# Filler products between the row groups of the first batch, and a softmax that works by rows of the score matrix

## The chip, the cores and the metric

The kernel runs on one core of one Trainium2 chip. The metric is the device time of one execution in microseconds (us), and the number given for a kernel is the median of its runs. A core has five engines with a queue of instructions each: TensorE (PE in the profile; its weight loads are listed apart as PEld), VectorE (DVE), ScalarE (ACT), GpSimd (POOL) and SyncE (SP). Each works through its queue in order and waits on semaphores for the others. Here POOL and SP do little but issue DMA transfers.

## The reference, cut to what matters

There are 4 batches of N = 6016 rows and C = 256 columns for each of q, k and v. Attention is between columns, not rows. After it comes a gated feed-forward layer with 1536 inner columns.

```
qn = q / (norm(q, axis=1) + 1e-6)        # one norm for each batch and column
kn = k / (norm(k, axis=1) + 1e-6)
s  = kn.T @ qn / tau                     # 256 x 256 for each batch, tau = 1
a  = exp(s - max(s));  a /= a.sum(-1) + 1e-9
x  = v @ a
out = (sigmoid(x @ w_gate) * (x @ w_val)) @ w_out
```

## The kernel before

**What is multiplied.** The kernel never forms x. Since x @ w_gate = v @ (a @ w_gate), it computes two small matrices for each batch, G = a @ w_gate and H = a @ w_val (256 x 1536 each). The large loop then multiplies the transposed v by G and H. The numerators of the softmax are held transposed in `x_sb` and `e_sb`: the partitions are columns of q, in two halves j of 128, and the free dimension is columns of k, in two blocks i of 128. A sum over a row of a is therefore a sum over partitions, made by PE with a vector of ones. The row maximum is replaced by the bound 1/tau.

**Rows.** The 6016 rows are 47 tiles of 128. Four tiles make a chunk, so a batch has 12 chunks (`ci` 0 to 11), the last one with 3 tiles. For the first batch, `groups0` has eleven groups of 4 tiles, then one of 2 and one of 1.

**The main loop** (L478 to L499) runs over batches b, chunks ci and twelve steps f. `glu` (L334) computes 128 inner columns for a whole chunk: two matmuls into `ps_gate`, two into `ps_val`, a sigmoid on ACT into `g_sb` (L353), and their product on DVE into `hT` (L354). The second matmul layer, `out_mms` (L360), lies one chunk behind: four of its matmuls follow each step, and after every twelfth `flush` (L376) copies a finished `ps_o` on DVE in the next step (L380). In chunks 9 and 10 of the first three batches ("block") these 48 matmuls come after the twelve steps instead of between them.

**Side work** (`side_work`, L433) is a table written by hand. While batch b runs, it gives the steps in which the pieces of batch b+1 are issued, after that step's `glu` and `out_mms`. The slot ci*12 + f names chunk and step. Loads and scores are spread over chunks 0 to 8. Then come, before the change: the norms' products in chunk 9, step 10, and the square root in step 11 (L462, L463); `norms_inv`, add and reciprocal on DVE, in chunk 10, step 1 (L464); two copies of the scores out of PSUM, `copy_s`, in step 2 (L466); `spread_k`, four PE products that lay the inverse norms of k along a row of `ps_rk`, in step 4 (L467); `scale_k` for both blocks in step 6 and `exps` in step 11 (L469, L470); `sums` for both blocks in chunk 11, step 0 (L471); and the twelve products `gh` (L292) in chunk 11, one in each of the steps 1 to 10 and two in step 11 (L474). A `gh` product is two matmuls into a `ps_gh`, then a copy out of PSUM that multiplies by the inverse row sum `rrow`, on ACT (L307) or DVE (L309).

**The softmax before.** `scale_k(b, i)` makes two DVE instructions of 128 columns, multiplying by both inverse norms: `r` (q, one for each partition) and `ps_rk` (k). `exps(b, i)` is one exp over both halves j of column block i. `sums(b, i)` is two matmuls with the ones into a `ps_r`, then an add (L280) and a reciprocal (L281) on DVE. The products are ordered by `gh_order` = (fg, i, w): fg is one of three groups of 512 inner columns, w is gate or val.

**PSUM.** There are eight buffers: psg 2 (`ps_gate`), psv 2 (`ps_val`), pso 2 (`ps_o`, `ps_rk`), pss 1 (scores) and psm 1 (norms and others). A tile that takes a buffer waits for the last reader of the tile before it. Sums and products of the side work alternate between psm and pss.

**The head** (L391 to L430). POOL's queue loads batch 0's groups of q and k, then v and the weights. For each group g come the squares, on DVE for q and ACT for k (exchanged for the last group), the scores, and then the norms' products of group g-1. `sqpool` holds two squares of each kind, so a square waits for the norms' products two groups back. After the last group come the square root, `norms_inv`, `copy_s`, twelve unread products by `busy` (L385: 128-column products of ones with ones, into a psg buffer), `spread_k`, four more, `scale_k` and `exps` for both blocks, the transposes of the first v chunk on PE, whose two halves DVE and ACT copy (L328, L329), and six `gh` products into psg, psv and pso. The other six follow the first six steps of chunk 0. `transpose_v(0, 1)` is also made on PE, in step 7 of chunk 0; all later chunks of v are transposed by DMA. A table load for exp (L405) and one for the sigmoid (L425) are placed by hand on ACT.

```
    for g in range(last0 + 2):
        if g <= last0:
            ...
            for u in range(nt):
                score(0, t0, u)
        if g >= 1:
            norm_mms(ps_n0, sq.pop(g - 1), groups0[g - 1][1], g == 1, g == last0 + 1, (0, 1) if g <= last0 else (1, 0))
```

Of the kernel before, what the change touches and what calls it, by code (L numbers as in the profile page):

```python
# [9 lines left out]
FP32 = mybir.dt.float32  # L10
BF16 = mybir.dt.bfloat16
# [6 lines left out]
def kernel(  # L18
# [68 lines left out]
    def mm(out, lhsT, rhs, start, stop, **kw):  # L87
        nc.tensor.matmul(out, lhsT=lhsT, rhs=rhs, start=start, stop=stop, **kw)  # L88
# [82 lines left out]
            )  # L171
        return sq

    def norm_mms(ps, sqs, nt, first, last, order=(0, 1)):

        for w in order:
            sq = sqs[w]
            for u in range(nt):
                for j in range(CB):
                    mm(  # L180
                        ps[:, w * CB + j : w * CB + j + 1],
                        sq[:, u, ds(j * P, P)],
                        ones_bf[:, 0:1],
                        start=(first and w == order[0] and u == 0 and j == 0),
                        stop=(last and u == nt - 1),
                        skip_group_check=True,
                    )
# [59 lines left out]
            s["x"] = attp.tile([P, CB, C], FP32, tag="x", name="x_sb")  # L247
        nc.vector.tensor_copy(out=s["x"][:, j, :], in_=s["s"][:, j, :])

    def scale_k(b, i):  # L250

        s = st[b]
        for j in range(CB):
            x = s["x"][:, j, ds(i * P, P)]
            nc.vector.scalar_tensor_tensor(  # L255
                out=x,
                in0=x,
                scalar=s["r"][:, j : j + 1],
                in1=s["rk"][:, ds(i * P, P)],
                op0=ALU.mult,  # L260
                op1=ALU.mult,
            )

    def exps(b, i):

        s = st[b]
        e = attp.tile([P, CB, P], BF16, tag=f"e{i}", name=f"e_sb{i}", bufs=2)
        nc.scalar.activation(  # L268
            out=e, in_=s["x"][:, :, ds(i * P, P)], func=ACT.Exp, bias=shift
        )  # L270
        s.setdefault("e", []).append(e)
        s.setdefault("rrow", [])

    def sums(b, i, pl=psm, tag="m"):
        s = st[b]
        ps_r = pl.tile([P, 1], FP32, tag=tag, name="ps_r")
        for j in range(CB):
            mm(ps_r, s["e"][i][:, j, :], ones_bf[:, 0:1], j == 0, j == CB - 1)
        r = attp.tile([P, 1], FP32, tag=f"rrow{i}", name="rrow", bufs=2)
        nc.vector.tensor_scalar(out=r, in0=ps_r, scalar1=1e-9, scalar2=None, op0=ALU.add)  # L280
        nc.vector.reciprocal(r, r)  # L281
        s["rrow"].append(r)

    def gh_tiles(b):
        st[b]["gh"] = [
            [ghpool.tile([P, CB, FG], BF16, tag=f"{n}{fg}", name=f"gh_{n}{fg}") for fg in range(NFG)]
            for n in ("G", "H")
        ]

    gh_order = [(fg, w, i) for fg in range(NFG) for i in range(CB) for w in range(2)]  # L290

    def gh(b, n, pl=None, tag=None, act=None):  # L292
        s = st[b]
        fg, w, i = gh_order[n]
        ps = (pl or psm).tile([P, FG], FP32, tag=tag or "m", name="ps_gh")
        for j in range(CB):
            mm(
                ps,
                s["e"][i][:, j, :],
                w_sb[w][fg][:, j, :],  # L300
                start=(j == 0),
                stop=(j == CB - 1),
            )
        dst = s["gh"][w][fg][:, i, :]
        r = s["rrow"][i]
        if act if act is not None else n % 2 == 0:
            nc.scalar.activation(out=dst, in_=ps, func=ACT.Copy, scale=r)  # L307
        else:
            nc.vector.tensor_scalar(out=dst, in0=ps, scalar1=r, scalar2=None, op0=ALU.mult)  # L309
# [1 line left out]

    vts = {}

    def transpose_v(b, ci, ps=None, late=None):

        t0, nt = groups[ci]
        v_sb = vs.pop((b, ci))
        vT = vtpool.tile([P, TPC * CB, P], BF16, tag="vT", name="vT")
        flat = v_sb[:, :nt, :].rearrange("p t c -> p (t c)")
        if ps is None:  # L320
            nc.sync.dma_start_transpose(out=vT[:, : nt * CB, :], in_=flat)
        else:
            for n in range(nt * CB):
                nc.tensor.transpose(
                    out=ps[:, n, :], in_=flat[:, ds(n * P, P)], identity=ident_bf
                )
            half = nt * CB // 2
            nc.vector.tensor_copy(out=vT[:, :half, :], in_=ps[:, :half, :])  # L328
            (nc.scalar.copy if late is None else late)(vT[:, half : nt * CB, :], ps[:, half : nt * CB, :])  # L329
        vts[b, ci] = vT.rearrange("p (u cb) n -> p cb u n", cb=CB)  # L330

    hts = {}
# [52 lines left out]
    def busy(n):  # L385

        ps = psg.tile([P, CH], FP32, tag="g", name="ps_busy")
        for _ in range(n):
            mm(ps[:, :P], ones_bf, ones_bf, True, True)

    ps_n0 = psm.tile([P, 2 * CB], FP32, tag="m", name="ps_n")  # L391
    sq = {}
    last0 = len(groups0) - 1
    for g in range(last0 + 2):
        if g <= last0:
            t0, nt = groups0[g]
            engines = (nc.vector, nc.scalar) if g < last0 else (nc.scalar, nc.vector)
            sq[g] = [squares(0, t0, nt, w, engines[w]) for w in range(2)]
            for u in range(nt):
                score(0, t0, u)  # L400
        if g >= 1:
            norm_mms(ps_n0, sq.pop(g - 1), groups0[g - 1][1], g == 1, g == last0 + 1, (0, 1) if g <= last0 else (1, 0))
    st[0]["n"] = ps_n0
    norms_sqrt(0)
    nc.scalar.preload_act_table(ACT.Exp)  # L405
# [2 lines left out]
    copy_s(0, 1)  # L408
    busy(12)
    spread_k(0)  # L410
    busy(4)
    scale_k(0, 0)
    scale_k(0, 1)
    late = []
    transpose_v(
        0, 0, psv.tile([P, TPC * CB, P], BF16, tag="v", name="ps_tp"), lambda *a: late.append(a)
    )
    exps(0, 0)
    exps(0, 1)
    nc.scalar.copy(*late.pop())  # L420
    gh_tiles(0)
    sums(0, 0)
    gh(0, 0, psg, "g", act=False)
    gh(0, 1, psv, "v", act=True)
    nc.scalar.preload_act_table(ACT.Sigmoid)  # L425
    sums(0, 1, pss, "s")
    gh(0, 2, psg, "g", act=False)
    gh(0, 3, psv, "v", act=False)
    gh(0, 4, pso, "o", act=True)
    gh(0, 5, pso, "o", act=False)  # L430


    def side_work(b):  # L433

        side = {}

        def at(slot, fn, *a):
            side.setdefault(divmod(slot, FC), []).append((fn, a))

        for ci in range(NCH):  # L440
            nb, nci = (b, ci + 1) if ci + 1 < NCH else (b + 1, 0)
            lb, lci = (b, ci + 2) if ci + 2 < NCH else (b + 1, ci + 2 - NCH)
            if (nb, nci) == (0, 1):
                at(7, lambda: transpose_v(0, 1, psm.tile([P, TPC * CB, P], BF16, tag="m", name="ps_tp")))
            elif nb < B:
                at(ci * FC + 2, transpose_v, nb, nci)
            if lb < B:
                at(ci * FC + 0, load_v, lb, lci)
        n = b + 1
        if n == B:  # L450
            return side
        first, last = (14 if b == 0 else 0), 9 * FC
        for g, (t0, nt) in enumerate(groups):
            s0 = first + g * (last - first) // NCH
            at(max(0, s0 - 20), load_qk, n, t0, nt)
            for u in range(nt):
                at(first + (t0 + u) * (last - first) // NT, score, n, t0, u)
            if g == 0:
                at(s0, acc_start, n)
            for i, (fn, w) in enumerate(((acc_square, 0), (acc_add, 0), (acc_square, 1), (acc_add, 1))):  # L460
                at(s0 + 1 + 2 * i, fn, n, g, w)
        at(9 * FC + 10, norms_mm, n)  # L462
        at(9 * FC + 11, norms_sqrt, n)  # L463
        at(10 * FC + 1, norms_inv, n)  # L464
        for j in range(CB):
            at(10 * FC + 2, copy_s, n, j)  # L466
        at(10 * FC + 4, spread_k, n)  # L467
        for i in range(CB):
            at(10 * FC + 6, scale_k, n, i)  # L469
            at(10 * FC + 11, exps, n, i)  # L470
            at(11 * FC + 0, sums, n, i, *((psm, "m"), (pss, "s"))[i])  # L471
        at(11 * FC + 0, gh_tiles, n)
        for i in range(len(gh_order)):
            at(11 * FC + min(i + 1, FC - 1), gh, n, i, *((psm, "m"), (pss, "s"))[i % 2])  # L474
        return side


# [1 line left out]
    for b in range(B):  # L479
        side = side_work(b)  # L480
        for ci in range(NCH):
            block = b + 1 < B and ci in (9, 10)
            for f in range(FC):
                glu(b, ci, f)
                flush()
                if prev is not None and not block:
                    out_mms(*prev, f * TPC, (f + 1) * TPC)
                for fn, a in side.get((ci, f), ()):
                    fn(*a)
                if (b, ci) == (0, 0) and f < len(gh_order) - 6:  # L490
                    gh(0, 6 + f, pso, "o")
            if prev is not None and block:
                for s in range(TPC):
                    out_mms(*prev, s * FC, (s + 1) * FC)
# [40 lines left out]
```

## Time and profile before

| | us |
|---|---|
| median of 3 runs (lowest, highest) | 834.85 (834.69, 836.2) |
| time of the profiled execution | 834.69 |
| its span | 832.8 |
| around the span | 1.9 |

The profile is of one execution. Its page has numbered parts: busy time of each engine; the span in 40 slices of 20.8 us; DMA queues; the chain of work that ended last; groups of equal instructions with mean duration and what their engine waited for; and DMA issues. Two rows of the second part:

```profile
PE   5899999999999999999999999999999999999998
...
DMA  9999623326655543223865453223222523322111
```

Each digit is a share in tenths: PE is less than full in the first two slices and the last, and the DMA engines are full in the first four. Besides the page, the trace answers questions by window. The timeline lists start, duration, engine, line, operation, written tile <- read tiles, shape and count, and in square brackets the idle time of the engine before it and what ended that. The ends of matmuls are modelled and overlap, so the pitch from start to start is the better measure of a stream of them.

### The profile page before, as it was taken

How to read it: one execution, taken by the hardware profiler on the slowest of the kernel's cores; microseconds unless marked ns; L12 is line 12 of the kernel's file. 1: busy time of each engine (PE TensorE's matmuls, PEld its weight loads, DVE VectorE, ACT ScalarE, POOL GpSimd, SP SyncE). 2: the span in 40 equal slices, each digit the busy share in tenths (PEclk: the TensorE clock that was granted, in tenths of full speed). 3: DMA queues.
4: the chain of work that ended last, by engine and by line, in shares of the span. 5: the costliest groups of instructions: out<-in, count | busy, mean ns of one | idle time of the engine just before them, and what ended most of it. 6: DMA issues, size and time to landing. Idle time of an engine off the chain costs nothing.

```text
span 832.8 us, 14005 instructions
## 1 busy us (share of the span) xinstructions
PE 813.2 (98%) x5322; PEld 506.0 (61%) x5332; DVE 568.6 (68%) x993; ACT 390.8 (47%) x642; POOL 82.9 (10%) x159
## 2 busy tenths in 40 slices
PE   5899999999999999999999999999999999999998
PEld 4656666665666666665576666666566566666666
DVE  2477777776667777777657777777766666666664
ACT  4554444445544444444654444444655444444442
POOL 5532100002011100000210020000000000000000
PEclk9799999999999999999999999999999999999999
DMA  9999623326655543223865453223222523322111
GB/s 209 206 206 185 130 52 89 61 52 130 133 102 108 102 106 57 58 52 83 156 130 103 84 113 78 51 75 65 61 48 64 83 51 82 71 48 70 45 35 71
DMA packets 78739, 77.19 MB, mean 93 GB/s; under 512 B 50768, under 2 KB 55632, under 8 KB 78672
## 3 DMA queue, kind: packets, MB, share of 16 engines
q0 software_dynamic: 23920, 38.81, 28.1%
q1 hardware_dynamic: 54608, 36.97, 17.0%
q8 instruction: 41, 0.67, 0.3%
q10 hardware_dynamic: 144, 0.52, 0.2%
q14 instruction: 26, 0.21, 0.1%
HBM read 78.64 MB, written 24.64 MB: 124 GB/s over the span
## 4 chain that ended last, share of the span: by engine, by line
PE 93%; DMA 4%; DVE 1%; issue 0%; POOL 0%; ACT 0%; POOLq 0%
PE ps_o L88 30%; PE ps_gate L88 29%; PE ps_val L88 29%; PE ps_s L88 4%; DMA k_sb<-in_k_dram 3%; PE ps_gh L88 2%; DMA w_val<-in_moe_w_val_dram 1%; DVE hT L354 1%; ACT g_sb L353 0%; DVE x_sb L255 0%; PE ps_rk L88 0%; PE ps_n L88 0%; POOL q_sb L97 0%; POOL w_gate L137 0%; POOL k_sb L97 0%
## 5 line engine op out<-in xcount | busy, mean ns | idle before, releaser
L354 DVE TENSOR_TENSOR hT<-ps_val,g_sb 128x512 bf16<-128x512 f32 (+1 forms) x576 | 390.9, 680 | 211.7 <-ACT g_sb L353 206.7
L353 ACT ACTIVATE g_sb<-ps_gate 128x512 bf16<-128x512 f32 (+1 forms) x576 | 338.5, 588 | 398.6 <-PE ps_gate L88 390.8
L88 PE MATMUL ps_val<-vT,gh_H 128*128 128x512 bf16 (+1 forms) x1152 | 337.8, 375 | 1.5 <-DVE hT L354 1.4
L88 PE MATMUL ps_gate<-vT,gh_G 128*128 128x512 bf16 (+1 forms) x1152 | 337.8, 375 | 0.6 <-ACT g_sb L353 0.3
L88 PE MATMUL ps_o<-w_out_sb,hT 128*128 128x256 bf16 x2256 | 326.4, 273 | 0.0
L88 PEld LDWEIGHTS <-hT 128*128 128x128 bf16 x2256 | 220.7, 98 | 124.8
L88 PEld LDWEIGHTS <-gh_H 128*128 128x128 bf16 x1152 | 112.7, 98 | 132.9 <-issue 2.6
L88 PEld LDWEIGHTS <-gh_G 128*128 128x128 bf16 x1152 | 112.2, 98 | 36.9 <-issue 0.5
L380 DVE COPY out_sb<-ps_o 128x256 f32<-128x256 f32 x188 | 78.2, 416 | 20.6 <-PE ps_o L88 20.6
L106 POOL DMA_DIRECT2D v_sb<-in_v_dram x48 | 25.5, 531 | 626.6 <-DMA vT<-v_sb 513.3
L88 PE MATMUL ps_s<-k_sb,q_sb 128*128 128x256 bf16 x376 | 71.8, 293 | 12.6 <-ACT k_sb L128 7.1
L88 PEld LDWEIGHTS <-q_sb 128*128 128x128 bf16 x376 | 39.1, 104 | 20.4 <-DVE q_sb L127 6.7
L208 DVE TENSOR_TENSOR acc<-acc,sq 128x1024 bf16<-128x1024 bf16 (+1 forms) x66 | 44.2, 670 | 0.0
L169 DVE TENSOR_TENSOR sq<-q_sb 128x1024 bf16<-128x1024 bf16 (+2 forms) x45 | 30.1, 670 | 19.0 <-PE ps_n L88 18.2
L97 POOL DMA_DIRECT2D q_sb<-in_q_dram x48 | 26.2, 547 | 15.7 <-DMA q_sb<-in_q_dram 6.7
L97 POOL DMA_DIRECT2D k_sb<-in_k_dram x48 | 26.4, 549 | 14.0 <-DMA k_sb<-in_k_dram 8.7
L169 DVE TENSOR_TENSOR sq<-k_sb 128x1024 bf16<-128x1024 bf16 (+2 forms) x34 | 22.4, 658 | 0.7 <-PE ps_n L88 0.7
L307 ACT ACTIVATE gh_G<-ps_gh,rrow 128x512 bf16<-128x512 f32 x22 | 15.1, 687 | 13.3 <-PE ps_gh L88 9.1
L167 ACT ACTIVATE sq<-k_sb 128x1024 bf16<-128x1024 bf16 (+1 forms) x12 | 12.3, 1021 | 14.8 <-DMA k_sb<-in_k_dram 12.9
L309 DVE TENSOR_SCALAR gh_H<-ps_gh,rrow 128x512 bf16<-128x512 f32 x23 | 17.1, 743 | 1.8 <-PE ps_gh L88 1.6
L88 PE MATMUL ps_gh<-w_val,e_sb 128*128 128x512 bf16 x45 | 13.6, 379 | 0.5 <-DMA w_val<-in_moe_w_val_dram 0.3
L88 PEld LDWEIGHTS <-e_sb 128*128 128x128 bf16 x112 | 10.1, 97 | 5.3 <-ACT e_sb L268 0.7
(49 smaller groups left out, 92.8 us busy)
## 6 DMA issues: line engine op xcount, KB each, us to landing
out_dram<-out_sb SPq DMA_DIRECT2D x44, 512.0 KB, 2.9
v_sb<-in_v_dram POOLq DMA_DIRECT2D x44, 256.0 KB, 3.8
q_sb<-in_q_dram POOLq DMA_DIRECT2D x43, 256.0 KB, 6.8
k_sb<-in_k_dram POOLq DMA_DIRECT2D x43, 256.0 KB, 7.7
out_dram<-out_sb SPq DMA_DIRECT2D x4, 384.0 KB, 2.5
w_gate<-in_moe_w_gate_dram POOLq DMA_DIRECT2D x3, 256.0 KB, 6.8
w_val<-in_moe_w_val_dram POOLq DMA_DIRECT2D x3, 256.0 KB, 7.4
w_out_sb<-in_moe_w_out_dram POOLq DMA_DIRECT2D x1, 768.0 KB, 12.6
```

The source lines that it names most:

```text
L88: nc.tensor.matmul(out, lhsT=lhsT, rhs=rhs, start=start, stop=stop, **kw)
L97: nc.gpsimd.dma_start(out=tl[:, :nt, :], in_=rows(src, b)[:, t0 : t0 + nt, :])
L106: nc.gpsimd.dma_start(out=v_sb[:, :nt, :], in_=rows(v, b)[:, t0 : t0 + nt, :])
L167: nc.scalar.activation(out=sq[:, :nt, :], in_=src[:, :nt, :], func=ACT.Square)
L169: engine.tensor_tensor(out=sq[:, :nt, :], in0=src[:, :nt, :], in1=src[:, :nt, :], op=ALU.mult)
L208: nc.vector.tensor_tensor(out=acc[:, :nt, :], in0=acc[:, :nt, :], in1=st[b]["sq", w][:, :nt, :], op=ALU.add)
L307: nc.scalar.activation(out=dst, in_=ps, func=ACT.Copy, scale=r)
L309: nc.vector.tensor_scalar(out=dst, in0=ps, scalar1=r, scalar2=None, op0=ALU.mult)
L353: nc.scalar.activation(out=g_sb[:, :n], in_=ps_gate[:, :n], func=ACT.Sigmoid)
L354: nc.vector.tensor_tensor(out=hts[b, ci][:, f, :n], in0=ps_val[:, :n], in1=g_sb[:, :n], op=ALU.mult)
L380: nc.vector.tensor_copy(out=out_sb[:, s, :], in_=ps)
```

## The change

It consists of these parts:

- **Filler in the head.** `busy(40)` stands ahead of the first group. In the group loop `busy(12)` follows the norms' products for g = 0 to 10. After `spread_k` there are ten such products instead of four.
- **Squares of the last group.** Both are on DVE. `norm_mms` loses its parameter for the order, and q always comes first.
- **Softmax by rows.** `scale_k` makes two DVE products of 256 columns with `ps_rk` alone. The inverse norms of q become the per-partition scale of `exps`, which makes one exp for each half j. The sums over a row need both halves; `sums` makes four matmuls into one psm tile, one add and one reciprocal, and takes over the allocation of G and H.
- **Order and buffers of the products.** `gh_order` is (fg, w, i). In the side work sums and products all use psm. In the head, four products precede the loop, into psg and psv, with odd ones copied on ACT; the other eight follow steps 0 to 7 of chunk 0.
- **Copies of the transposed v** in chunks 0 and 1 of batch 0 are one DVE copy.
- **Slots of the side work.** `spread_k` moves from step 4 to 2, `copy_s` from 2 to 1 and `scale_k` from 6 to 4 of chunk 10; product n goes from step n+1 to n of chunk 11.

```diff
-            norm_mms(ps_n0, sq.pop(g - 1), groups0[g - 1][1], g == 1, g == last0 + 1, (0, 1) if g <= last0 else (1, 0))
+            norm_mms(ps_n0, sq.pop(g - 1), groups0[g - 1][1], g == 1, g == last0 + 1)
+        if g < NT // TPC:
+            busy(12)
...
+    def scale_k(b):
         s = st[b]
         for j in range(CB):
+            x = s["x"][:, j, :]
+            nc.vector.tensor_tensor(out=x, in0=x, in1=s["rk"], op=ALU.mult)
+
+    def exps(b):
+        s = st[b]
+        s["e"] = attp.tile([P, CB, C], BF16, tag="e", name="e_sb", bufs=2)
         for j in range(CB):
+            nc.scalar.activation(
+                out=s["e"][:, j, :],
+                in_=s["x"][:, j, :],
+                func=ACT.Exp,
+                bias=shift,
+                scale=s["r"][:, j : j + 1],
+            )
+
+    def sums(b):
+        s = st[b]
+        ps_r = psm.tile([P, CB], FP32, tag="m", name="ps_r")
+        for i in range(CB):
+            for j in range(CB):
+                mm(
+                    ps_r[:, i : i + 1],
+                    s["e"][:, j, ds(i * P, P)],
+                    ones_bf[:, 0:1],
+                    start=(i == 0 and j == 0),
+                    stop=(j == CB - 1),
+                    skip_group_check=True,
+                )
+        r = attp.tile([P, CB], FP32, tag="rrow", name="rrow", bufs=2)
         nc.vector.tensor_scalar(out=r, in0=ps_r, scalar1=1e-9, scalar2=None, op0=ALU.add)
         nc.vector.reciprocal(r, r)
...
-    gh_order = [(fg, w, i) for fg in range(NFG) for i in range(CB) for w in range(2)]
+    gh_order = [(fg, w, i) for fg in range(NFG) for w in range(2) for i in range(CB)]
...
-            half = nt * CB // 2
-            nc.vector.tensor_copy(out=vT[:, :half, :], in_=ps[:, :half, :])
-            (nc.scalar.copy if late is None else late)(vT[:, half : nt * CB, :], ps[:, half : nt * CB, :])
+            nc.vector.tensor_copy(out=vT[:, : nt * CB, :], in_=ps[:, : nt * CB, :])
...
+    busy(40)
     ps_n0 = psm.tile([P, 2 * CB], FP32, tag="m", name="ps_n")
...
-            engines = (nc.vector, nc.scalar) if g < last0 else (nc.scalar, nc.vector)
-            sq[g] = [squares(0, t0, nt, w, engines[w]) for w in range(2)]
+            sq[g] = (
+                squares(0, t0, nt, 0, nc.vector),
+                squares(0, t0, nt, 1, nc.vector if g == last0 else nc.scalar),
+            )
...
-    busy(4)
-    scale_k(0, 0)
-    scale_k(0, 1)
...
+    busy(10)
+    scale_k(0)
+    transpose_v(0, 0, psv.tile([P, TPC * CB, P], BF16, tag="v", name="ps_tp"))
+    exps(0)
     nc.scalar.preload_act_table(ACT.Sigmoid)
-    sums(0, 1, pss, "s")
-    gh(0, 2, psg, "g", act=False)
-    gh(0, 3, psv, "v", act=False)
-    gh(0, 4, pso, "o", act=True)
-    gh(0, 5, pso, "o", act=False)
+    sums(0)
+    for n in range(4):
+        gh(0, n, *((psg, "g"), (psv, "v"))[n % 2], act=1)
...
+        at(10 * FC + 2, spread_k, n)
         for j in range(CB):
-            at(10 * FC + 2, copy_s, n, j)
-        at(10 * FC + 4, spread_k, n)
-        for i in range(CB):
-            at(10 * FC + 6, scale_k, n, i)
-            at(10 * FC + 11, exps, n, i)
-            at(11 * FC + 0, sums, n, i, *((psm, "m"), (pss, "s"))[i])
-        at(11 * FC + 0, gh_tiles, n)
+            at(10 * FC + 1, copy_s, n, j)
+        at(10 * FC + 4, scale_k, n)
+        at(10 * FC + 11, exps, n)
+        at(11 * FC + 0, sums, n)
         for i in range(len(gh_order)):
-            at(11 * FC + min(i + 1, FC - 1), gh, n, i, *((psm, "m"), (pss, "s"))[i % 2])
+            at(11 * FC + i, gh, n, i)
...
-                if (b, ci) == (0, 0) and f < len(gh_order) - 6:
-                    gh(0, 6 + f, pso, "o")
+                if (b, ci) == (0, 0) and f < len(gh_order) - 4:
+                    gh(0, 4 + f, pso, "o", act=1)
```

## The prediction

> **What bounds the kernel now.** I read the page's first two parts, then the list of PE's waits, then PE's busy time in stretches of 3.41 us, then the timeline of the first 55 us and of the change from batch 0 to batch 1.
>
> ```profile
> PE 813.2 (98%) x5322; PEld 506.0 (61%) x5332; DVE 568.6 (68%) x993; ACT 390.8 (47%) x642; POOL 82.9 (10%) x159
> ...
> PEclk9799999999999999999999999999999999999999
> ```
>
> TensorE (PE) is busy in 98% of the span, so a moment in which it waits is added to the time. The granted clock is below full only in the first two slices. PE's own waits, as total, count and longest:
>
> ```profile
> PE ps_s L88 <- ACT k_sb L128: 7.1, 1, 7.1
> PE ps_s L88 <- DMA k_sb<-in_k_dram: 5.5, 8, 2.1
> PE ps_val L88 <- DVE hT L354: 1.4, 3, 0.5
> ```
>
> Up to 32 us PE waits for loads of k. The third row is one wait at each batch change. Now PE in stretches of 3.41 us (busy us, count, granted clock, DMA share, GB/s); the clock changes only at their edges:
>
> ```profile
> 10.09:13.50 3.41, 2.25 (x45) 0.99 1.13 211
> 13.50:16.91 3.41, 3.15 (x30) 0.51 1.12 209
> ...
> 20.33:23.74 3.41, 1.82 (x13) 0.50 1.12 208
> 23.74:27.15 3.41, 2.94 (x43) 0.50 1.12 209
> 27.15:30.57 3.42, 3.15 (x30) 0.51 1.13 207
> 30.57:33.98 3.41, 2.85 (x59) 1.00 1.24 204
> ```
>
> After a full-clock stretch with 2.25 us busy the clock halves. After half-clock stretches with 3.15 us it comes back, after 2.94 it did not, and at full clock 2.85 us kept it. The data rate is 207 to 211 GB/s in both states: the loads set the pace, not the clock. The last stretch begins warm, before the last full group of k lands:
>
> ```profile
> 31.94 1.03 PE L88 MATMUL ps_s<-k_sb,q_sb 128*128 128x256 bf16 x8 [0.56 <-DMA k_sb<-in_k_dram]
> 32.81 0.54 PE L88 MATMUL ps_n<-ones_bf,sq 128*128 128x1 bf16 x16
> 33.29 0.60 PE L88 MATMUL ps_s<-k_sb,q_sb 128*128 128x256 bf16 x4
> ...
> 34.82 0.83 PE L88 MATMUL ps_busy<-ones_bf 128*128 128x128 bf16 x12
> ...
> 37.65 0.20 PE L88 MATMUL ps_r<-ones_bf,e_sb 128*128 128x1 bf16 x2 [0.57 <-ACT e_sb L268]
> ...
> 40.81 0.59 PE L88 MATMUL ps_gate<-vT,gh_G 128*128 128x512 bf16 x2
> ```
>
> From 31.94 to 34.96 PE works without a gap, and its end releases square root, inverse norms, scaling, exp, sums and products. This is the path that matters in the head.
>
> **Fill in the head.** The 40 first products run between the memset of the ones (ends 1.01) and the first scores (7.05). At the cold pace (16 scores of 256 columns in 3.35 us, so 0.105 us for 128 columns) they take 4.2 us and are over by 5.4: nothing. Twelve products warm: the row above shows 0.83 us with the pipeline's tail, its weight loads 0.68; I take 0.68. After groups 0 to 9 they lie under the loads: scores 0.87, norms 0.48 and fill 0.68 make 2.03 us, and k groups land every 2.5 us. Without that cover (half clock) the three are 1.7 + 0.6 + 1.28 = 3.6 us, more than 2.5. After group 10 there is no cover: the short group's k was there by 33.29, and its scores follow 0.68 us later: **+0.68**. The gain in clock is worth nothing, because the groups that ran cold were waiting for loads and the last ones already ran warm.
>
> The Trainium skill, "TensorE: Matmul & The Clock Gate", section "Why this matters for your kernels", says that the clock halves after PE-idle gaps above about 3 us; by it this head, with no gap over 2.2 us after its start, would stay warm, fill would hold a clock that nothing threatens, and the sum would keep its 0.68 with no gain either. The rows differ: the clock halved at 13.50 with no gap above 1.2 us, so I go by busy time per stretch.
>
> **Softmax of batch 0.** The last squares (two on DVE instead of one each on ACT and DVE) end no later: q's norm products, which free its buffer, come first, so q's square (0.29) is done when k's may start. scale_k was 4 instructions at a pitch of 0.28, exp started 0.64 after the first. The new form, 128x256 in f32 with one PSUM operand, isn't in the trace: below it is the 128x128 row (0.34), above the 128x384 product of L354 (0.56); between 384 and 512 (0.56 and 0.69) the slope is 1.05 ns a column, giving 0.42, pitch 0.37. So exp starts 0.20 sooner. But sums need both exps, where sums of block 0 needed one: a step later, 0.50 by the exp row, 0.59 if a scale read from memory costs what it seems to in gh's copy (0.687 against the sigmoid's 0.597); I take 0.59. Sums move from 37.65 to 37.65 + 0.68 - 0.20 + 0.64 (0.59 and 0.05 for its longer first exp) = 38.77. The transposed v's whole copy on DVE (one half is 0.42, so 0.42 to 0.84) lies under the exps; if not, it delays the sums' add by up to 0.3.
>
> ACT then loads the sigmoid table (1.28, L425) before its first product copy, where before it copied first: exps end 38.78, table 40.06, copies of products 1 and 3 (0.69 each) 40.75 and 41.44. gate(0) isn't held up by more than 0.1; val(0)'s second half waits for product 3 and ends about 41.70. Product 4 follows, step 1 starts at 42.13 with 5 products done; before it started at 42.10 with 7. Two products are 0.86: together **+0.89**, fill included. The 0.29 us that product 5 waited for w_val at 40.38 goes within this; what is late next is ACT.
>
> Inside the first chunk product 7 now comes directly before glu(4), product 11 before glu(8). A product's copy ends 1.32 after its matmul starts (41.67 to 42.99); val's second half would need it at 0.43 + 0.43 + 0.22 = 1.08: 0.28 twice, 0.56. Against that ACT no longer copies half of the second v tile: gates and vals near 52.9 and 53.6 lost 0.42 + 0.30 = 0.72. Head in all: 0.89 + 0.56 - 0.72 = **+0.73**.
>
> **The three batch changes.** All columns as before; chunk 10 starts at 205.97, chunk 11 at 222.63.
>
> ```profile
> 208.90 0.18 DVE L225 RECIPROCAL r<-r 128x4 f32<-128x4 f32 x1
> ...
> 210.29 0.61 PE L88 MATMUL ps_rk<-ident_f,r 128*128 128x128 f32 x4
> ...
> 215.23 0.59 PE L88 MATMUL ps_val<-vT,gh_H 128*128 128x512 bf16 x2 [0.45 <-DVE hT L354]
> ...
> 223.71 0.24 PE L88 MATMUL ps_r<-ones_bf,e_sb 128*128 128x1 bf16 x4
> ...
> 224.15 0.15 DVE L280 TENSOR_SCALAR rrow<-ps_r 128x1 f32<-128x1 f32 x1
> ```
>
> spread_k moves from step 4 to step 2. PE gets there at 208.56, the reciprocal ends at 209.08, and in the head PE followed it by 0.11: 209.19. Unhidden weight loads (0.52 against a pitch of 0.44) bring the stall to **0.70**; queued behind it is glu(3). The copies of s, a step earlier, fall into that stall. scale_k on DVE takes 2 x 0.37 instead of 4 x 0.26, so the stall that now shows at 215.23 (0.61 in pace) becomes 0.32. Chunk 10: 0.70 + 0.32 - 0.61 = **+0.41**.
>
> In chunk 11, sums and every product share psm's one buffer, where sums and products alternated between psm and pss. Product 0 follows sums in step 0: PE is there at 223.82, but DVE's add, behind hT(0), frees the buffer at 224.30, so 224.37: **+0.55**. Later products follow each other by 1.51 us. An ACT copy ends 1.32 after its product starts, a DVE copy 1.43: under 1.51 (margins 0.2 and about 0.03). Where an output copy stands ahead on DVE it is later:
>
> ```profile
> 232.49 0.38 PE L88 MATMUL ps_gh<-w_val,e_sb 128*128 128x512 bf16 x1
> ...
> 233.51 0.74 DVE L309 TENSOR_SCALAR gh_H<-ps_gh,rrow 128x512 bf16<-128x512 f32 x1
> ```
>
> That is 1.76 to the end, 1.82 with the release: 0.31 late, which meets steps 3 and 9: **+0.62**. Order (fg, w, i) and the missing second product of step 11 cost nothing: fg 0 is done seven steps before use. POOL's and SP's issues stay in their steps; their loads land chunks ahead.
>
> A change costs 0.41 + 0.55 + 0.62 = 1.58; three cost 4.74.
>
> **Sum.** The profiled execution took 834.69 (span 832.8 and 1.9 around it); the median is 0.16 more. 834.69 + 0.73 + 4.74 = 840.16, on the median's scale **840.3 us**.
>
> **Rivals.**
> 1. *The fill goes cold and falls behind.* At 20.38 the filled PE would wait 1.54 us for the k group that landed at 21.92. That leaves 1.9 us busy in a stretch, below 2.25, so half clock from 23.74. Group 7 starts at 24.46, the stretch to 27.15 has 2.9 busy (2.94 didn't recover), and groups 7 and 8 at 3.6 us each push group 10 from 31.94 to about 33.2: +1.2, **841.5**. For it: that gap and those rows. Against: another phase of the stretches recovers at once. This is also the case that the change doesn't hold the clock as it says.
> 2. *Half of the new waits.* If buffer waits in chunk 11 are covered (tile released sooner than I count), 834.85 + 0.73 + 3 x 0.41 = 836.8; with half of them 838.5. Against: the add stands behind hT(0) on DVE.
> 3. *Not slower: DVE is ahead of PE where PE asks.* Place: step 2 of chunk 10, steps 0, 3 and 9 of chunk 11. It decides if the reciprocal ends before 208.56 and the add before 223.82, a lead of 0.5 to 0.6 us. Then only the shorter scale_k remains, -0.3 x 3, with the head's 0.73: **834.7**. Against: DVE's share near there is 0.5 to 0.8 and it waits for the sigmoid of the same step, so it cannot lead.
>
> **Chances.** Forecast 0.51 (own range 838.9 to 841.2), rival 1 0.25, rival 2 0.15, rival 3 0.09. 0.2% is about what a measurement of this kernel can tell from no change, 1.67 us. Only rival 3 lies within it: 0.06 same, 0.03 faster, 0.91 slower. The range 836.8 to 842.8 takes in rivals 1 and 2, the scale_k and exp bounds, the DVE margin of 0.03 missing nine times by 0.1, and leaves out rival 3 and a fill later than 1.2 us.
>
> **What would show it.** Right: clock 1.0 from 10 us on; ps_busy between ps_n and the 4-score row after 31.94; ps_rk waiting on DVE r for about 0.6 at each change; ps_gh waiting on rrow once and on gh copies twice in chunk 11; ps_val's wait shorter. Wrong: no PE wait in 208 to 209 or 223 to 239, or scores of group 10 later than 32.0 without a later load.

## The result, and the profile after

| us | before | after |
|---|---|---|
| median (lowest, highest; 6 runs each) | 834.77 (834.38, 836.2) | 839.49 (839.43, 839.55) |
| span of the profiled execution | 832.8 | 837.4 |

The ratio is 1.0052, with a 95% interval from 1.0039 to 1.0065: the changed kernel is slower by about 4.7 us. The prediction was 840.3, so its sign, size and range were right; one of its terms, the filler, was more than twice too large, and one of its reasons, what sets the clock, was wrong. The runs of the changed kernel lie within 0.12 us of each other; those of the kernel before spread over 1.8 us.

The page of the changed kernel, its first part and the granted clock:

```profile
PE 821.7 (98%) x5499; PEld 514.2 (61%) x5510; DVE 566.4 (68%) x977; ACT 390.4 (47%) x640; POOL 83.0 (10%) x159
...
PEclk9999999999999999999999999999999999999999
```

PE has gained 8.5 us of busy time, chiefly from 13.5 more in filler rows and 5.6 less in score rows, which no longer run at half clock. The clock row is full throughout. PE's waits (total, count, longest):

```profile
PE ps_s L88 <- DMA k_sb<-in_k_dram: 4.4, 9, 1.3
...
PE ps_rk L88 <- DVE r L224: 1.2, 3, 0.4
PE ps_gh L88 <- DVE rrow L281: 1.2, 3, 0.4
```

The loads of k still hold PE up. The wait of ps_val on hT has left the list, and two waits that didn't exist before have come, three times each, once at each batch change.

The head, in the timeline:

```profile
31.66 1.03 PE L88 MATMUL ps_s<-k_sb,q_sb 128*128 128x256 bf16 x8 [0.36 <-DMA k_sb<-in_k_dram]
...
32.53 0.54 PE L88 MATMUL ps_n<-ones_bf,sq 128*128 128x1 bf16 x16
...
32.93 0.83 PE L88 MATMUL ps_busy<-ones_bf 128*128 128x128 bf16 x12
33.28 0.63 ACT L167 ACTIVATE sq<-k_sb 128x512 bf16<-128x512 bf16 x1 [0.51 <-DMA k_sb<-in_k_dram]
...
33.60 0.60 PE L88 MATMUL ps_s<-k_sb,q_sb 128*128 128x256 bf16 x4
...
40.71 0.76 PE L88 MATMUL ps_val<-vT,gh_H 128*128 128x512 bf16 x2
...
46.05 0.90 PE L88 MATMUL ps_val<-vT,gh_H 128*128 128x512 bf16 x2
```

The filler after group 10 is where it was expected, but ACT's square, which waits for the same load as the next scores, shows that this load came only at 33.28. The last row is a pair of matmuls that takes 0.90 instead of 0.59: its second half waits for product 7.

The first batch change, from two stretches of the timeline:

```profile
209.29 0.18 DVE L224 RECIPROCAL r<-r 128x4 f32<-128x4 f32 x1
...
209.53 0.71 PE L88 MATMUL ps_rk<-ident_f,r 128*128 128x128 f32 x4 [0.41 <-DVE r L224]
...
214.20 0.59 PE L88 MATMUL ps_val<-vT,gh_H 128*128 128x512 bf16 x2
...
224.85 0.15 DVE L281 TENSOR_SCALAR rrow<-ps_r 128x2 f32<-128x2 f32 x1
...
225.05 0.38 PE L88 MATMUL ps_gh<-w_gate,e_sb 128*128 128x512 bf16 x1 [0.40 <-DVE rrow L281]
```

```profile
230.29 0.41 DVE L377 COPY out_sb<-ps_o 128x256 f32<-128x256 f32 x1
...
230.63 0.74 DVE L308 TENSOR_SCALAR gh_H<-ps_gh,rrow 128x512 bf16<-128x512 f32 x1
...
231.42 0.59 PE L88 MATMUL ps_gh<-w_gate,e_sb 128*128 128x512 bf16 x2
```

ps_rk starts after the reciprocal, product 0 after the add, and product 4 only when DVE's copy of product 3, behind an output copy (L377), has ended (231.37). The bracketed times are shorter than what is lost, since modelled ends of matmuls overlap the wait. Pitches of starts give the loss. Where the time came from, by the start of the same matmul in both traces:

| first gate matmul of | before | after | later by | added since |
|---|---|---|---|---|
| step 11, chunk 0, batch 0 | 54.05 | 54.45 | 0.40 | 0.40 |
| chunk 10, batch 0 | 205.97 | 206.37 | 0.40 | 0 |
| chunk 11, batch 0 | 222.63 | 223.33 | 0.70 | 0.30 |
| chunk 0, batch 1 | 240.95 | 242.77 | 1.82 | 1.12 |

Head 0.40 and three times 1.42 make 4.66; the spans differ by 4.6.

### The profile page after: what moved, and what is told of

The parts are those of the page before. It is cut to its first block, busy times and chain, and to the rows that moved or that the text cites. A ratio compares the mean times of both kernels' runs of the same rounds, so it can differ in the third digit from the quotient of the medians.

```text
span 837.4 us, 14334 instructions
## 1 busy us (share of the span) xinstructions
PE 821.7 (98%) x5499; PEld 514.2 (61%) x5510; DVE 566.4 (68%) x977; ACT 390.4 (47%) x640; POOL 83.0 (10%) x159
## 4 chain that ended last, share of the span: by engine, by line
PE 91%; DMA 3%; DVE 2%; ACT 1%; issue 1%; POOL 0%; ACTq 0%; POOLq 0%
PE ps_o L88 29%; PE ps_gate L88 28%; PE ps_val L88 28%; PE ps_s L88 4%; DMA k_sb<-in_k_dram 3%; PE ps_gh L88 2%; DVE hT L351 1%; ACT g_sb L350 1%; PE ps_rk L88 0%; DVE out_sb L377 0%; ACT gh_H L306 0%; PE ps_n L88 0%; DVE gh_H L308 0%; DVE gh_G L308 0%; DVE x_sb L253 0%
## 5 line engine op out<-in xcount | busy, mean ns | idle before, releaser
L377 DVE COPY out_sb<-ps_o 128x256 f32<-128x256 f32 x188 | 78.3, 416 | 20.9 <-PE ps_o L88 20.9
L88 PE MATMUL ps_s<-k_sb,q_sb 128*128 128x256 bf16 x376 | 66.2, 272 | 6.1 <-DMA k_sb<-in_k_dram 4.4
L169 DVE TENSOR_TENSOR sq<-q_sb 128x1024 bf16<-128x1024 bf16 (+3 forms) x46 | 30.4, 662 | 20.2 <-PE ps_n L88 11.8
L88 PEld LDWEIGHTS <-q_sb 128*128 128x128 bf16 x376 | 36.6, 98 | 12.1 <-issue 5.6
L88 PE MATMUL ps_busy<-ones_bf 128*128 128x128 bf16 x194 | 14.7, 234 | 1.1 <-DVE shift L125 1.1
L88 PE MATMUL ps_gh<-w_gate,e_sb 128*128 128x512 bf16 x41 | 12.7, 378 | 1.7 <-DVE rrow L281 1.2
```

Of the source, the lines that this page charges most:

```text
L169: engine.tensor_tensor(out=sq[:, :nt, :], in0=src[:, :nt, :], in1=src[:, :nt, :], op=ALU.mult)
L377: nc.vector.tensor_copy(out=out_sb[:, s, :], in_=ps)
```

## The experiments

Theory: the new time is three waits at each batch change (ps_rk on the reciprocal, product 0 on the add, products 4 and 10 on a copy in psm's one buffer) and little in the head, where filler hides behind loads. Rivals: the filler itself costs, or gains; or DVE would stall PE there whatever the buffers and steps. The comparisons had their own runs of the kernel before, between 834.28 and 836.61, with medians from 834.91 to 835.57. That spread is itself one of the things to explain.

**Filler alone, with and without the twelve after group 10**, in the kernel before:

```diff
+    busy(40)
     ps_n0 = psm.tile([P, 2 * CB], FP32, tag="m", name="ps_n")
...
+        if g < NT // TPC:          # second kernel: NT // TPC - 1
+            busy(12)
```

> The kernel before with the filler alone: 40 products ahead of the first group and 12 after the norms' products of groups 0 to 10. My theory: only the 12 after group 10 lie on the path, so 0.68 us over the kernel before (834.8 to 835.5 in the median), the granted clock at 1.0 through the head, and runs that agree within 0.3 us. Rival 1, a warm clock shortens the head: under 834.4. Rival 2, the filler falls behind the loads: over 836.

> The kernel before with 40 products ahead of the first group and 12 after groups 0 to 9, none after group 10. My theory: all of it is covered by the loads, so the time of the kernel before when its head runs well, 834.4 to 834.9, and none of the runs near 836.1 that the kernel before shows in 2 of 6, if those come from the phase of the clock. Rival 1 (warm clock shortens the head): 833.8 or less. Rival 2 (runs near 836 have another cause): they appear here too.

Measured: 834.88 (834.75 to 835.0, ratio 0.9996, 0.9987 to 1.0005) with the last twelve and 834.72 (834.63 to 834.96, ratio 0.9997, 0.9988 to 1.0006) without. So the last twelve cost about 0.16, not 0.68. The timelines, first of the kernel with them, then without:

```profile
32.86 0.83 PE L88 MATMUL ps_busy<-ones_bf 128*128 128x128 bf16 x12
33.53 0.60 PE L88 MATMUL ps_s<-k_sb,q_sb 128*128 128x256 bf16 x4
```

```profile
33.36 0.60 PE L88 MATMUL ps_s<-k_sb,q_sb 128*128 128x256 bf16 x4 [0.51 <-DMA k_sb<-in_k_dram]
```

Without filler the same scores wait for their load until 33.36. In this pair of traces the load covers most of the twelve. Neither rival holds for the median. All 22 runs stay below 835.1, whereas the kernel before reaches 836.5 in the same comparison: filler doesn't make the head shorter than the head before at its best, it makes it repeat.

**Two buffers for the products** of the changed kernel:

```diff
-            at(11 * FC + i, gh, n, i)
+            at(11 * FC + i, gh, n, i, *((pss, "s"), (psm, "m"))[i % 2])
```

> The changed kernel, with the side work's products alternating between pss and psm, sums in psm. My theory: the waits at products 0, 4 and 10 of each batch change (0.53 + 0.30 + 0.30 in the changed kernel's trace) go, three times 1.13 = 3.4, so 836.1. Rival: the waits come from products a step earlier or from DVE being late with what they need, not from the buffer: 838.5 to 839.5.

Measured 836.26 (ratio to the kernel before 1.0013, 1.0004 to 1.0022), 3.23 below the changed kernel. ps_gh's wait on rrow has left the list of waits, and chunk 11 takes 18.33 us (223.38 to 241.71) as in the kernel before (18.32), against 19.44 in the changed one. The products stay a step earlier in this run, so the buffer was the cause and not the step.

**spread_k and scale_k later**, `copy_s` left in step 1:

```diff
-        at(10 * FC + 2, spread_k, n)
-        at(10 * FC + 4, scale_k, n)
+        at(10 * FC + 4, spread_k, n)
+        at(10 * FC + 6, scale_k, n)
```

> The changed kernel, with spread_k back in step 4 and scale_k in step 6 of chunk 10, copy_s left in step 1. My theory: the stall at ps_rk (0.67) goes three times, the stall behind scale_k (0.24) stays, so 2.0 less: 837.5. Rival: DVE's backlog from the copies, not the reciprocal, holds PE there, and another stall takes its place: 838.8 to 839.5.

Measured 839.1 (838.95 to 839.67; ratio 1.0047, 1.0033 to 1.0061): a miss, only 0.4 gained. The rival had the price and half of the reason: PE did wait for the reciprocal, and another stall took that wait's place. The timeline:

```profile
209.35 0.72 DVE L247 COPY x_sb<-ps_s 128x256 f32<-128x256 f32 x2
...
210.73 0.59 PE L88 MATMUL ps_val<-vT,gh_H 128*128 128x512 bf16 x2 [0.35 <-DVE hT L351]
```

ps_rk doesn't wait any more. But the copies, which now follow the inverse norms in the same step, put the next hT on DVE back by 0.64 (to 209.99, from the 209.35 at which they start), so val(4) has to wait for its buffer and starts at 210.73 instead of 210.21. So a second experiment moved the copies too.

**All three back in their old steps**, which adds one line to the edit above:

```diff
-            at(10 * FC + 1, copy_s, n, j)
+            at(10 * FC + 2, copy_s, n, j)
```

> The changed kernel with copy_s, spread_k and scale_k in steps 2, 4 and 6 of chunk 10 as before; psm alone as in the change. My theory after the run with spread_k in step 4 and the copies left in step 1 (a stall of 0.52 at ps_val took the place of ps_rk's wait): both have to move, and then 0.67 goes three times, 837.5. Rival: the copies stall val wherever they are, 838.9 to 839.5.

Measured 837.55 (ratio 1.0026, 1.0016 to 1.0036), 1.94 below the changed kernel; chunk 10 takes 16.29 us (206.54 to 222.83), against 16.96 after and 16.66 before. So the copies moved alone cost 0.52 in each chunk 10, and moved together with spread_k they cost 0.67 once, not the sum of two stalls. A move of spread_k alone, with the copies in their old step, wasn't run.

**Three things undone:** two buffers for the products, the old steps, and no filler after group 10.

```diff
-        if g < NT // TPC:
+        if g < NT // TPC - 1:
             busy(12)
...
-        at(10 * FC + 2, spread_k, n)
+        at(10 * FC + 4, spread_k, n)
         for j in range(CB):
-            at(10 * FC + 1, copy_s, n, j)
-        at(10 * FC + 4, scale_k, n)
+            at(10 * FC + 2, copy_s, n, j)
+        at(10 * FC + 6, scale_k, n)
...
-            at(11 * FC + i, gh, n, i)
+            at(11 * FC + i, gh, n, i, *((pss, "s"), (psm, "m"))[i % 2])
```

> The changed kernel with three things undone: products alternate between pss and psm, copy_s, spread_k and scale_k are in steps 2, 4 and 6 as in the kernel before, and there is no filler after group 10. What stays of the change is the filler after groups 0 to 9, the softmax by rows, the order of products and the whole copies of v. My theory: the changed kernel's 839.5 less 3.25 (two buffers, measured), 2.0 (ps_rk's wait without the copies that take its place) and 0.2 (filler): 834.1. Rival: softmax by rows is dear by itself (its sums wait for both exps, its products for ACT's table) or the steps give back less: 835.5 to 836.

Measured 833.85 (833.71 to 834.21; ratio 0.9984, 0.9975 to 0.9993). So what is left of the change isn't dear: step 11 of chunk 0 starts at 54.03 (before: 54.05), and chunk 10 takes 16.29, 0.37 less than before, because scale_k's two instructions hold DVE for less time than four. Three times 0.37 is 1.1; the span is 831.6 against 832.8.

**A version that beats both:** the kernel before, with filler after groups 0 to 9, and with two stalls taken away that its own trace shows.

```diff
-            at(10 * FC + 6, scale_k, n, i)
+            for j in range(CB):
+                at(10 * FC + 5 + 2 * i + j, scale_k, n, i, (j,))
...
-            half = nt * CB // 2
+            half = nt * CB // 2 if late is not None else nt * CB
```

(With `late` unset, ACT's copy of the second half is dropped too; `scale_k` takes the halves j to do.)

> The kernel before with filler after groups 0 to 9, scale_k's four instructions spread over steps 5 to 8 of chunk 10, and DVE alone copying the second v tile. My theory: the stall behind scale_k (0.61 in pace) goes three times, and of the 0.72 lost near 52.9 and 53.6 some 0.45 goes: 834.7 less 1.8 less 0.45, 832.4. Rival: DVE has no room for pieces either, four small stalls take the place of one: 834 to 834.7.

Measured 832.15 (831.96 to 832.28; ratio 0.9961, 0.9948 to 0.9973). Its timeline at the batch change:

```profile
211.82 0.34 DVE L255 SCALAR_TENSOR_TENSOR x_sb<-x_sb,r,ps_rk 128x128 f32<-128x128 f32 x1
212.08 0.69 DVE L355 TENSOR_TENSOR hT<-ps_val,g_sb 128x512 bf16<-128x512 f32 x1
```

Each piece sits ahead of one hT and puts it back by less than val can bear; no ps_val wait is left. Chunk 10 takes 16.05 us, 0.61 less than before, and step 11 of chunk 0 starts at 53.27, 0.78 sooner.

**A head that meets its end at half clock:** the scores of groups 1 to 9 are left out.

```diff
-                score(0, t0, u)
+                if not 1 <= g <= 9:
+                    score(0, t0, u)
```

> The kernel before without the scores of groups 1 to 9 of batch 0 (left out, so batch 0's part of the output is not the reference's). PE is then busy for about 0.5 us in 2.5 while the loads run, and meets the last full group with a half clock. My theory: the last stretch at half clock costs 1.4 to 3 us, 836.2 to 838, and this is what the slower ones of the kernel before's own runs show. Rival: the last stretch waits for loads so much that the clock makes no difference: 834.4 to 835.

Measured 835.92 (835.3 to 836.91; ratio 1.0008, 0.9998 to 1.0017), a little under what was expected. PE's timeline:

```profile
31.54 1.87 PE L88 MATMUL ps_s<-k_sb,q_sb 128*128 128x256 bf16 x8 [3.46 <-DMA k_sb<-in_k_dram]
...
42.28 0.59 PE L88 MATMUL ps_gate<-vT,gh_G 128*128 128x512 bf16 x2
```

The eight scores take 1.87 instead of 1.03, and the first gate matmul starts at 42.28, 1.47 later than in the kernel before, and the span is 834.5, 1.7 more. So a head that ends at half clock costs about 1.5 us against the short execution of the kernel before that was profiled, which is of the size of that kernel's spread; against its median (835.33 in this comparison) the difference isn't clear. That its own longer executions are such heads is the natural reading. Their clocks fit: of its 67 runs in the three comparisons, the 15 at 836.0 and above had a mean granted clock of 0.988 to 0.990, and none with 0.991 or more took over 835.9. But some of 834.3 had 0.990 too, and no long run was profiled, so it isn't shown where in the head they lost their time.

**How much filler holds the clock:** 6 and 2 products instead of 12, after groups 0 to 9.

```diff
         if g < NT // TPC - 1:
-            busy(12)
+            busy(6)                    # second kernel: busy(2)
```

> The kernel before with 40 products ahead of the first group and 6 after groups 0 to 9. In the traces so far the clock fell after stretches of 3.41 us in which PE streamed 3104 to 3456 columns, and stayed or came back with 3584 and more, whatever the rows' busy time was. By columns: a group is 8 x 256 + 16 + 6 x 128 = 2832 in 2.5 us, 3870 in a stretch: the clock holds from its first rise on, but for a stretch with a late load. By the rows' busy time (fell at 2.25 us in the kernel before): 2.6 to 2.7 us, undecided. Time 834.4 to 835.0.

> The same with 2 products after groups 0 to 9. By columns: 2320 in 2.5 us, 3170 in a stretch, below 3456, so the clock falls in the head as it does in the kernel before. If instead it is the length of a gap without products that counts, which is shorter here than in the kernel before by 0.11 us only, or if any filler will do, the clock holds. Time 834.3 to 836.5, spread as in the kernel before.

Measured 834.43 (834.33 to 834.53; ratio 0.9985, 0.9973 to 0.9996) with 6 and 834.94 (834.3 to 835.53; ratio 0.9993, 0.9981 to 1.0004) with 2. With 6 the clock fell once, after a late load. Stretches of PE (busy us, count, clock, DMA share, GB/s):

```profile
12.83:16.24 3.41, 1.77 (x30) 0.99 1.12 210
16.24:19.65 3.41, 2.96 (x32) 0.50 1.12 210
19.65:23.06 3.41, 3.41 (x35) 0.51 1.13 210
23.07:26.48 3.41, 2.94 (x57) 1.00 1.12 211
```

With 2 it fell three times between 5 and 33 us, and the last time it came back only at 32.58, inside the stretch that matters; the runs scatter again:

```profile
12.10:15.51 3.41, 2.48 (x48) 1.00 1.12 211
15.51:18.92 3.41, 1.55 (x26) 0.99 1.11 207
...
25.75:29.16 3.41, 1.60 (x27) 0.99 1.13 210
29.16:32.57 3.41, 3.41 (x31) 0.50 1.22 202
```

That 6 holds the clock but for a late load, and that 2 doesn't, is as the count of columns said. With 2 the reason was only half right: 3170 is an average, the stretches that the clock fell after held fewer (2320 in the one from 15.51), and the one from 12.10 kept the clock with what the average promised. One group with its norms' products and 6 of filler is 2832 columns, with 12 it is 3600, and a late load can leave a stretch one group: with 6 the clock then fell (from 12.83), with 12 it stayed. In time 6 were enough here, and the twelve after each group weren't needed.

## Why the prediction was right, point by point

- **What bounds the kernel** was read rightly: PE's own waits add to the time. Head 0.40 and three times 1.42 account for the whole difference.
- **Filler, +0.68: the mis-sized term.** The step that failed is "after group 10 there is no cover". The short group's k was there by 33.29, as the prediction says, but only just: in the trace of the kernel before, its load was issued at 24.7 and landed 8.5 us later, at 33.2. In the five traces with twelve products after group 10 it landed between 33.2 and 33.6, and its scores began between 33.53 and 33.66, so part of the twelve lay under it, and in one trace nearly all. Counted from that load, the filler's end at 33.60 is 0.3 to 0.4 late in the changed kernel, and 0.16 is the difference of the medians with and without. I took the last full group as the start of the path without asking when the next load was due. That group 10 itself began 0.28 sooner in the changed kernel's execution doesn't follow from the filler: it began at 31.43 to 31.94 in the twelve traces, with filler and without.
- **"The gain in clock is worth nothing"** holds against the best runs of the kernel before (834.28 against 834.33 and 834.63, the lowest with 6 and 12 products). It leaves out the rest: the runs up to 836.6 are gone, and the median with 6 products is 1.1 below that of the kernel before beside it (834.43 against 835.57).
- **Softmax of batch 0** was right: the two scalings took 0.75 together, exp began 0.46 after the first of them began (0.44 expected), and the sums could go on 1.15 after exp began (1.20 expected: 0.56 as before and 0.64 more). ACT's table was late as said: product 1's copy began at 39.57 and val(0)'s pair took 0.76.
- **The first chunk** was right: val(4) and val(8) lost 0.30 and 0.31 (0.28 each expected), and the 0.72 near 53 us went. Head in all 0.40 against 0.73; the filler, 0.3 instead of 0.68, is the difference.
- **Chunk 10, +0.41**: measured 0.30. The stall at ps_rk was 0.67 (0.70 expected), that behind scale_k 0.24 (0.32). One sentence was true and yet misleading: the copies did "fall into that stall", but they were not free. Without it they cost 0.52 of their own, which putting spread_k and scale_k back alone brought to light.
- **Chunk 11, +1.17**: measured 1.12, as 0.53, 0.30 and 0.30; the DVE copies with a margin of 0.03 all met it. Undoing the single buffer gave 3.23 back (3.4 expected).
- **Rival 1** (filler goes cold and falls behind) didn't come, and its condition was wrong: I took busy time, "below 2.25, so half clock". Two stretches of the changed kernel had less and the clock stayed full:

```profile
4.56:7.97 3.41, 1.74 (x23) 1.00 1.11 235
...
14.80:18.21 3.41, 2.07 (x39) 1.00 1.12 210
```

  The fall that it feared came with filler of 6, and even there the head recovered before group 10.
- **Rivals 2 and 3** (waits covered; DVE ahead of PE) are refuted by the two bracketed waits and by the runs that undid them.

## What to carry to other kernels

When a kernel is bound by one engine, price a reordering of its side work by who must have finished at the new place: here one buffer in place of two and a step or two of haste cost over ten times what the filler did. Undo one move at a time and then both, since one stall can hide another of nearly its size. Filler for the clock belongs under a load that is still due, and six products a group were enough here, two weren't; what it buys is a time that repeats, not a shorter best time.

## What the runs showed of the hardware

The clock of TensorE changes only at the edges of stretches of 3.41 us, and in these traces it goes by the columns streamed in the stretch before, not by the busy time of the rows: 128x1 products fill rows but stream almost nothing. Columns are counts times width. A matmul that an edge cuts is counted whole in the first column of numbers, and in the second by its part inside, with the edges of the trace's own record of the clock, 0.04 us before the starts given here.

| kernel, start of stretch (us) | columns, whole | by part | busy us | clock in the next |
|---|---|---|---|---|
| filler of 2, 15.51 | 2320 | 2320 | 1.55 | half |
| before, 23.74 | 2848 | 2321 | 2.94 | half |
| before, 10.09 | 3360 | 2764 | 2.25 | half |
| filler of 12 (to group 10), 4.15 | 3456 | 3039 | 1.48 | half |
| filler of 6, 16.24 | 3344 | 3077 | 2.96 | half |
| filler of 12 (to group 9), 32.50 | 3242 | 3110 | 2.70 | full |
| filler of 2, 12.10 | 3616 | 3211 | 2.48 | full |
| before, 13.50 | 3600 | 3266 | 3.15 | full |
| filler of 12 (to group 9), 15.43 | 3600 | 3600 | 2.10 | full |
| after, 4.56 | 3968 | 3625 | 1.74 | full |

Counted whole, the stretch from 32.50 is out of order: it kept the full clock with 3242, where 3456 gave half. Counted by part, the order holds in all twelve traces, for the 114 stretches from each trace's first change of clock that start before 40 us: up to 3077 columns gave half clock next and 3110 or more full clock, whichever clock the stretch itself had. That is about 39% of what a full-clock stretch can stream (eight products of 256 columns take 0.87 us, which makes some 8000). The level is an estimate, since a few matmul records are missing and the edges matter. That the columns decide is an association over these stretches, used beforehand for the fillers of 6 and 2; no run moved them alone across the level.

The Trainium skill, "TensorE: Matmul & The Clock Gate", Part 1, has a free-running window of about 3.4 us, which the traces bear out: the first change comes at 10.1 us in the kernel before and at 4.5 in the changed one, and the others follow whole stretches later. Its advice in "Why this matters for your kernels" is to have no idle gaps above about 3 us, and that was not enough here: in the stretch from 10.09 no gap was above 1.2 us and the clock fell.

And a caution for reading such pages: before the first change of clock that a trace holds, the page prints full speed, but in the run without scores the eight scores at 31.54 took 1.87 us where the page says 1.00; the pace of the rows tells the true clock.
